# A padded tile that moves later tiles by 32 bytes, and the second token half's T sums split into an early and a late part

## The chip, the cores and the metric

The kernel runs on one core of a Trainium2 chip. The metric is the time of one execution on the device in microseconds (us). In what follows PE is TensorE, DVE is VectorE, ACT is ScalarE, POOL is GpSimd and SP is SyncE, whose queue issues all DMAs here.

## What is computed

```python
attn_out = _attn_ref(q, k, v, proj)          # (2, 8, 768, 64): attention masked by equal hash buckets
x = attn_out.transpose(0, 2, 1, 3).reshape(1536, 512)
g = h * tanh(softplus(h)),  h = x @ w_in     # moe_: 512 -> 2048 -> 512
x = g @ w_out
# moe2_: 8 experts, 512 -> 1024 -> 512, all tokens through all experts
P = exp(logits - max);  8 rounds of row and column normalisation (1536 x 8)
for e in range(8):
    out += P[:, e:e+1] * (max(x @ w1[e], 0) @ w2[e])
```

All in float32. The kernel gets float32 accuracy from TensorE's fp32r format by splitting each operand into a high part (rounded to fp32r) and a low part (the rest), and by summing three products: high x high, high x low, low x high.

## The kernel before

**Three stages.** The attention comes first (some 300 us) and is not touched. Then come the *blocks* (lines 760 to 1082): the first MLP and expert 0 of the second one, 72 steps `n` of 512 tokens by 128 hidden columns. In each step `up` (lines 785 to 787) issues 12 matmuls with 512 moving columns (stationary: a weight tile from a ring of eight, moving: `xh` and `xl`, the activations' high and low part), and `down` (L821) 12 more with the hidden tile `gh` or `gl` as one operand and the weight tile as the other. Last come the *units* (lines 1085 to 1226), `NU` = 56 of them: 28 for the first half of the tokens (g = 0), 28 for the second (g = 1), four for each of the experts 1 to 7. A unit computes a 2 x 2 block product by seven products instead of eight (Strassen's scheme in Winograd's form).

**A unit** has seven slots `s`. In slot `s`, `product(u, s)` issues six matmuls with 384 moving columns (L1111): weight sums S1 to S4 or weight blocks A as the stationary operand, token sums T1 to T4 or token blocks B (parts of `xh`, `xl`) as the moving one. After it comes a seventh of the 36 matmuls with 512 columns of the unit before (L1174, `second_mm`: stationary hidden tiles `gh`, `gl`, moving the second weights, `w` in even units and `ww` in odd ones). Then `post(u, s)` takes the products out of PSUM: DVE makes `u` after slot 1, `v` after slot 3, and `c` (L1131) after slots 4, 5 and 6; ACT rounds (`gh`, L1119), DVE makes `gl` (L1124). Two PSUM banks serve the seven products, so product 3 must wait for `u`, product 6 for the `c` of slot 4.

**Side work** is written into the slots by hand with `job(u, s, ...)` (and into the blocks' steps with `at(n, ...)`); each engine takes its instructions in the order written. For the next unit's weights POOL makes the four sums S (`unit_s`, four instructions) after slot 1, their low part (`unit_s_lo`, L1004) after slot 3, and the low part of A (`unit_a_lo`, L986 and L987) after slot 4; `unit_w_lo` (L1011) comes after slot 0. ACT makes the high parts (`..._hi`). All weights of even units go to ring tiles 0 to 2, those of odd units to `ws`, `wa`, `ww`.

**The T sums** are made by `make_t(g, k, kc, tmp)` (lines 956 to 974): three to five DVE instructions on 128 x 384 tiles in SBUF, then ACT's rounding (L973), then DVE's low part (L974). Eight calls serve a token half (k = 1 to 4, kc = 0, 1). For g = 0 they stand in the blocks' steps 61 to 68, in the midst of the normalisation rounds (steps 58 to 66; DVE's L882 to L897, PE's column sum `cs` L892 once per step). For g = 1 they stand in unit 25 (k = 2: slots 0 and 3), unit 27 (k = 3: slots 3 and 4; k = 1: slots 4 and 5; the first of k = 4: slot 6) and unit 28 (the second of k = 4: slot 0). T2 of g = 1 goes into a part of `xh`, `xl` that nobody reads any more; T1, T3 and T4 overwrite those of g = 0, which unit 27 still reads.

**Where the tiles lie.** Tiles are laid out one after another, a pool on top of the other. `fold` (L764, 32 bytes in each partition) is followed by all the tiles that the blocks and units open. In the built program `xh`, `xl`, the ring's tiles 0 to 2, `acc` and `tw` (the T sums) begin 32 bytes past a multiple of 64; the ring's tiles 3 to 7, all `gh` and `gl`, and `ws`, `wa`, `ww` begin at a multiple of 64. So the two operands of a matmul have the same offset in some places and different ones in others:

| matmuls | stationary | moving | count |
|---|---|---|---|
| `up`, ring tiles 0 to 2 | 32 | 32 | 27 x 12 |
| `up`, ring tiles 3 to 7 | 0 | 32 | 45 x 12 |
| `down`, ring tiles 3 to 7 | 0 | 0 | 45 x 12 |
| `down`, ring tiles 0 to 2 | 32 or 0 | 0 or 32 | 27 x 12 |
| products of even units | 32 | 32 | 28 x 42 |
| products of odd units | 0 | 32 | 28 x 42 |
| `second_mm`, weights of even units (issued in odd units) | 0 | 32 | 28 x 36 |
| `second_mm`, weights of odd units (issued in even units) | 0 | 0 | 28 x 36 |

Of the kernel before, what the change touches and what calls it, by code (L numbers as in the profile page):

```python
# [7 lines left out]
F32 = mybir.dt.float32  # L8
# [8 lines left out]
P = 128  # L17
# [5 lines left out]
E = 8  # L23
# [34 lines left out]
def lsh_attention_moe_kernel(  # L58
# [704 lines left out]
    NT = NTOK // P  # L763
    fold = acc_p.tile([2 * E, E], F32, name="fold")  # L764
    nc.vector.tensor_add(fold, idt[0:2 * E, 0:E], idt[0:2 * E, E:2 * E])
# [189 lines left out]

    def make_t(g, k, kc, tmp):
        n1, n2 = tokens(g, 0), tokens(g, 1)
        h, l = f32(xh), f32(xl)
        a, b = tmp(), tmp()
        if k < 4:  # L960
            p, q = ((kc, n2), (kc, n1)) if k < 3 else ((KC // 2 + kc, n2), (kc, n2))
            nc.vector.tensor_sub(a, h[:, p[0], p[1]], h[:, q[0], q[1]])
            nc.vector.tensor_sub(b, l[:, p[0], p[1]], l[:, q[0], q[1]])
            nc.vector.tensor_add(a, a, b)
        else:
            t = [factor_t(g, 2, m, kc).bitcast(F32) for m in range(2)]
# [22 lines left out]

    def unit_s(u, r):  # L990
        t = staged["u", u, 0]
        a11, a12, a21, a22 = t[:, 0, 0:256], t[:, 0, 256:512], t[:, 1, 0:256], t[:, 1, 256:512]
        nc.gpsimd.tensor_add(r[:, 0:256], a21, a22)
        nc.gpsimd.tensor_sub(r[:, 256:512], r[:, 0:256], a11)
        nc.gpsimd.tensor_sub(r[:, 512:768], a11, a21)
        nc.gpsimd.tensor_sub(r[:, 768:1024], a12, r[:, 256:512])
        box["s"] = r

    def unit_s_hi(u):
        nc.scalar.copy(wbuf[u % 2]["s"][:, 0, :], box["s"])  # L1000
# [14 lines left out]
    t0 = start_e + 12  # L1015
    at(t0, open_t)
    for x in range(8):
        at(t0 + 1 + x, make_t, 0, 1 + x // 2, x % 2, lambda: t_p.tile([P, TB], F32, tag="t", name="t")[:, :HALF])
    raw = lambda: t_p.tile([P, 1024], F32, tag="s", name="s", bufs=1)
    at(t0 + 3, unit_a_hi, 0)  # L1020
    at(t0 + 3, lambda: unit_s(0, raw()))
    at(t0 + 4, unit_s_hi, 0)
    at(t0 + 4, unit_s_lo, 0)
    at(t0 + 5, unit_a_lo, 0)
    at(t0 + 6, unit_w_hi, 0)
    at(t0 + 6, unit_w_lo, 0)

    free = {}
# [50 lines left out]
    pool = lambda name, **kw: ctx.enter_context(tc.tile_pool(name=name, reuse_waits="tile", **kw))  # L1079
    wb_p, c_p, h_p, s_p = pool("wb", bufs=1), pool("c", bufs=1), pool("hid", bufs=2), pool("sraw", bufs=1)  # L1080
    ps_u = pool("ps_u", bufs=1, space=bass.MemoryType.PSUM)
# [113 lines left out]
    for u in range(NU):  # L1195
# [3 lines left out]
        if u + 1 < NU:  # L1199
            job(u, 1, lambda u=u: unit_s(u + 1, s_p.tile([P, 1024], F32, tag="s", name="s")))  # L1200
            job(u, 2, unit_a_hi, u + 1)
# [3 lines left out]
    for i in range(NT):  # L1205
        job(i // 3, 1 + 2 * (i % 3), scale_first, i)
    half = NU // 2
    for x, (u, s) in enumerate(((-3, 0), (-3, 3), (-1, 3), (-1, 4), (-1, 4), (-1, 5), (-1, 6), (0, 0))):
        job(half + u, s, make_t, 1, (2, 3, 1, 4)[x // 2], x % 2, lambda: temp("t", 2))

# [72 lines left out]
```

## Time and profile before

| | |
|---|---|
| median of 3 runs | 1626.85 us (1626.85 to 1627.24) |
| the profiled execution | 1627.34 us, its span 1625.6 us |
| mean granted clock of TensorE | 0.986 of full speed |
| PE busy | 1569.6 us, 97% of the span |
| DVE, ACT, POOL busy | 871.3, 642.1, 865.2 us |
| share of the chain of waits that ended last: PE, DVE | 83%, 12% |

The span runs from the first instruction to the last; the rest of the execution's time (1.7 us) lies around it. A row of the timeline gives start, duration, engine, source line, operation, tile written <- tiles read, shapes, and in brackets how long the engine had been idle and what ended that. Matmuls overlap, so their pace is read from the difference of two starts and not from a duration.

### The profile page before, as it was taken

To read this page: it belongs to the slowest core of one execution; us is meant where nothing else is said; L and a number is where in the kernel's file an instruction comes from. 1 tells how busy PE (TensorE), PEld (TensorE's weight loads), DVE (VectorE), ACT (ScalarE), POOL (GpSimd) and SP (SyncE) were. 2 spreads that over 40 slices of the span, in tenths; PEclk is the share of its full clock that TensorE was granted. 3 is DMA by queue.
4 is the path that set the end of the run, shared out by engine and by line. 5 is a ranking of instruction groups with operands and counts; after the bars stand their busy time and mean duration, and the time that the engine had idled before them with its cause. 6 is when DMAs were issued, how large, how long until landed. Compare 5 with 4: busy or idle time off the path is not lost.

```text
span 1625.6 us, 20042 instructions
## 1 busy us (share of the span) xinstructions
PE 1569.6 (97%) x7407; PEld 1342.2 (83%) x7407; DVE 871.3 (54%) x1495; ACT 642.1 (40%) x1171; POOL 865.2 (53%) x694
## 2 busy tenths in 40 slices
PE   7888999999999999999999999998799999999999
PEld 5676787788888778788888888887688898888887
DVE  7999988677884222755433424336633334343343
ACT  4676776544333322223333333333333333333331
POOL 4778666432324240126666666665556666656663
PEclk7999999999999999999999999999999999999999
DMA  6755441022222010002122221222122222222221
GB/s 142 172 135 128 132 115 45 27 65 65 66 65 66 13 52 1 14 13 78 66 65 66 66 77 66 65 65 65 52 91 72 70 67 65 66 66 67 76 65 39
DMA packets 62641, 113.44 MB, mean 70 GB/s; under 512 B 18176, under 2 KB 18920, under 8 KB 62544
## 3 DMA queue, kind: packets, MB, share of 16 engines
q1 hardware_dynamic: 62544, 112.17, 23.7%
q8 instruction: 58, 0.95, 0.2%
q14 instruction: 39, 0.32, 0.1%
HBM read 89.22 MB, written 3.15 MB: 57 GB/s over the span
## 4 chain that ended last, share of the span: by engine, by line
PE 83%; DVE 12%; issue 1%; DMA 1%; ACT 1%; POOL 1%; SPq 0%; DVEq 0%; ACTq 0%; POOLq 0%
PE y L1174 28%; PE u L1111 24%; PE y L821 12%; PE h L785 4%; PE h L787 4%; PE h L786 4%; PE pav L487 3%; DVE mx L399 3%; PE ps L385 1%; PE pst L437 1%; PE pst L438 1%; DVE xu L516 1%; DVE col L404 1%; DVE vs L354 1%; DVE ph L446 0%
## 5 line engine op out<-in xcount | busy, mean ns | idle before, releaser
L1174 PE MATMUL y<-w,gh 128*128 128x512 f32 x672 | 220.9, 396 | 0.0
L1174 PE MATMUL y<-ww,gh 128*128 128x512 f32 x672 | 219.5, 395 | 0.0
L1119 ACT ACTIVATE gh<-c 128x384 fp32r<-128x384 f32 x168 | 88.3, 526 | 273.6 <-DVE c L1131 273.6
L449 POOL TENSOR_TENSOR plo<-p,ph 128x384 fp32r<-128x384 f32 x128 | 140.2, 1107 | 71.1 <-ACT ph L446 42.1
L1011 POOL TENSOR_TENSOR w<-stage,w 128x1024 fp32r<-128x1024 f32 x28 | 67.2, 2401 | 147.7 <-ACT w L1007 147.7
L1174 PEld LDWEIGHTS y<-ww,gh 128*128 128x128 f32 x672 | 125.9, 189 | 17.9
L1174 PEld LDWEIGHTS y<-w,gh 128*128 128x128 f32 x672 | 125.3, 188 | 18.2
L1011 POOL TENSOR_TENSOR ww<-stage,ww 128x1024 fp32r<-128x1024 f32 x28 | 67.5, 2409 | 127.2 <-ACT ww L1007 127.2
L1174 PE MATMUL y<-w,gl 128*128 128x512 f32 x336 | 132.9, 396 | 0.0
L1174 PE MATMUL y<-ww,gl 128*128 128x512 f32 x336 | 132.5, 394 | 0.0
L1004 POOL TENSOR_TENSOR w<-s,w 128x1024 fp32r<-128x1024 f32 x28 | 67.1, 2397 | 111.9 <-ACT w L1000 111.9
L157 POOL TENSOR_TENSOR stage<-stage,sgn 128x512 f32<-128x512 f32 x32 | 44.8, 1399 | 138.8 <-DVE sgn L155 57.3
L821 PE MATMUL y<-gh,w 128*128 128x512 f32 x336 | 111.5, 393 | 0.0
L1131 DVE TENSOR_TENSOR u<-u,p 128x384 f32<-128x384 f32 x56 | 31.2, 557 | 145.1 <-PE u L1111 145.1
L443 ACT ACTIVATE p<-pst 128x384 f32<-128x384 f32 x192 | 91.9, 488 | 42.4 <-PE pst L438 37.4
L787 PE MATMUL h<-xh,w 128*128 128x512 f32 x252 | 101.0, 401 | 2.6 <-POOL w L176 2.6
L785 PE MATMUL h<-xh,w 128*128 128x512 f32 x252 | 101.9, 405 | 0.0
L786 PE MATMUL h<-xl,w 128*128 128x512 f32 x252 | 101.0, 401 | 0.0
L399 DVE TENSOR_REDUCE mx<-ps 128x1 f32<-128x768 f32 x95 | 89.9, 946 | 17.2 <-PE ps L385 16.5
L1124 DVE SCALAR_TENSOR_TENSOR gl<-c,gh 128x384 fp32r<-128x384 f32 x168 | 96.1, 572 | 5.4
L1111 PE MATMUL u<-tw,w 128*128 128x384 f32 x420 | 86.2, 341 | 4.7 <-DVE u L1131 4.5
L1119 ACT ACTIVATE gh<-u 128x384 fp32r<-128x384 f32 x56 | 27.5, 491 | 157.1 <-PE u L1111 157.1
(244 smaller groups left out, 4004.9 us busy)
## 6 DMA issues: line engine op xcount, KB each, us to landing
stage<-in_w_dram SPq DMA_DIRECT2D x152, 512.0 KB
raw<-in_qk_dram SPq DMA_DIRECT2D x13, 384.0 KB
wx<-hi SPq DMA_DIRECT2D x20, 192.0 KB
vt<-in_v_dram SPq DMA_DIRECT2D x16, 192.0 KB
out_dram<-acc SPq DMA_DIRECT2D x12, 256.0 KB
zq<-hi SPq DMA_DIRECT2D x11, 192.0 KB
ak<-hi SPq DMA_DIRECT2D x11, 192.0 KB
zq<-lo SPq DMA_DIRECT2D x11, 192.0 KB
```

The costliest lines, as they stand in the source:

```text
L399: nc.vector.tensor_reduce(out=m[:, t:t + 1], in_=s_t[t][:, :, :HALF], axis=AX.XY, op=ALU.max)
L443: nc.scalar.activation(p_t[u, c], st_t.pop((u, c))[:, :HALF], AF.Exp, scale=0.125)
L449: (nc.gpsimd if e == "P" else nc.vector).tensor_sub(out, in0, in1)
L785: nc.tensor.matmul(t, wt[:, 0, f], xh[:, kc, c], start=(kc == 0), stop=False)
L786: nc.tensor.matmul(t, wt[:, 0, f], xl[:, kc, c], start=False, stop=False)
L787: nc.tensor.matmul(t, wt[:, 1, f], xh[:, kc, c], start=False, stop=(kc == KC - 1))
L821: nc.tensor.matmul(yps[j], x, y, start=(head and m == 0), stop=(tail and m == 2))
L1011: nc.gpsimd.tensor_sub(y[:, 1, :], t, f32(y)[:, 0, :])
L1111: nc.tensor.matmul(bank[x], weight(u, a, m, kc), moving(u, b, mm, kc), start=(first and n == 0), stop=(n == 5), skip_group_check=not first)
L1119: nc.scalar.activation(hi, src, AF.Relu)
L1124: nc.vector.scalar_tensor_tensor(out=lo, in0=src, scalar=0.0, in1=f32(hid_u[u, c][0]), op0=ALU.max, op1=ALU.subtract)
L1174: nc.tensor.matmul(y_t[t], (hi, hi, lo)[m][:, t % 3 * P:(t % 3 + 1) * P], y, start=(k == 0 and first and m == 0), stop=(k == NF // 2 - 1 a ...
```

## The change

`fold` is allocated 64 bytes wide and used in its first 32, so all that follows it begins 32 bytes later; one tile `sraw` takes the place of two tiles for the raw S sums. In the built program every tile of the table above then begins 32 bytes past a multiple of 64. `make_t` is cut into `raw_t` (the sum, on DVE) and `parts_t` (ACT's high, DVE's low part). For g = 1 the raw sums are made one per unit, in slot 3 of units 18 to 25; for k = 2 the parts follow at once (units 18, 19), for the other six the sum is held in a tile of its own, and the parts are made in unit 27 (slots 4, 5, 6) and 28 (slots 0, 1, 2). For g = 0 the eight calls stand three steps later in the blocks (64 to 71 for 61 to 68). The S sums of unit 1 move from slot 1 of unit 0 to step 69 of the blocks.

```diff
-    fold = acc_p.tile([2 * E, E], F32, name="fold")
+    fold = acc_p.tile([2 * E, 2 * E], F32, name="fold")[:, 0:E]
+    sraw = acc_p.tile([P, 1024], F32, name="sraw")
...
-    def make_t(g, k, kc, tmp):
+    def raw_t(g, k, kc, a, b):
...
+    def parts_t(g, k, kc, a):
         hi, lo = (factor_t(g, k, m, kc) for m in range(2))
         nc.scalar.copy(hi, a)
         nc.vector.tensor_sub(lo, a, hi.bitcast(F32))
...
+    def make_t(g, k, kc, tmp):
+        a = tmp()
+        raw_t(g, k, kc, a, tmp())
+        parts_t(g, k, kc, a)
+
     for x in range(8):
-        at(t0 + 1 + x, make_t, 0, 1 + x // 2, x % 2, ...)
+        at(t0 + 4 + x, make_t, 0, 1 + x // 2, x % 2, ...)
...
+    at(t0 + 9, unit_s, 1)
...
-            job(u, 1, lambda u=u: unit_s(u + 1, s_p.tile([P, 1024], F32, tag="s", name="s")))
+            if u:
+                job(u, 1, unit_s, u + 1)
...
-    for x, (u, s) in enumerate(((-3, 0), (-3, 3), (-1, 3), (-1, 4), (-1, 4), (-1, 5), (-1, 6), (0, 0))):
-        job(half + u, s, make_t, 1, (2, 3, 1, 4)[x // 2], x % 2, lambda: temp("t", 2))
+    held = {}
+
+    def raw_next(k, kc):
+        held[k, kc] = temp(f"t{k}{kc}" if k != 2 else "t")
+        raw_t(1, k, kc, held[k, kc], temp("tt"))
+        if k == 2:
+            parts_t(1, k, kc, held.pop((k, kc)))
+
+    def parts_next(k, kc):
+        parts_t(1, k, kc, held.pop((k, kc)))
+
+    for x in range(8):
+        job(half - 10 + x, 3, raw_next, (2, 3, 1, 4)[x // 2], x % 2)
+    for x, (u, s) in enumerate(((-1, 4), (-1, 5), (-1, 6), (0, 0), (0, 1), (0, 2))):
+        job(half + u, s, parts_next, (3, 1, 4)[x // 2], x % 2)
```

**DVE in unit 27, slots 3 to 5, before.** `v` and the `c`s are the sums that release PE's next products; `t` and `tw` belong to the T sums.

```order
L1131 TENSOR_TENSOR v<-u,p_10225 128x384
L962 TENSOR_TENSOR t<-xh 128x384
L963 TENSOR_TENSOR t<-xl 128x384
L964 TENSOR_TENSOR t<-t 128x384
L974 TENSOR_TENSOR tw<-t,tw 128x384
L1131 TENSOR_TENSOR c<-u,v 128x384
...
L1131 TENSOR_TENSOR c<-u,p_10225 128x384
L1124 SCALAR_TENSOR_TENSOR gl<-c,gh 128x384
```

At the "..." stand two more T sums whole, eight instructions. With the change the same place reads:

```order
L1139 TENSOR_TENSOR v<-u,p_10225 128x384
L1139 TENSOR_TENSOR c<-u,v 128x384
L977 TENSOR_TENSOR tw<-t_9352,tw 128x384
L1139 TENSOR_TENSOR c<-u,p_10225 128x384
L1132 SCALAR_TENSOR_TENSOR gl<-c,gh 128x384
L977 TENSOR_TENSOR tw<-t_9494,tw 128x384
L1139 TENSOR_TENSOR c<-u 128x384
```

One low part stands after each `c`, where up to eight instructions stood between two.

**DVE in units 18 and 20, slot 3, with the change** (k = 2, then k = 3; `t_9352` is the held sum):

```order
L1139 TENSOR_TENSOR v<-u,p_9028 128x384
L963 TENSOR_TENSOR t<-xh 128x384
L964 TENSOR_TENSOR tt<-xl 128x384
L965 TENSOR_TENSOR t<-t,tt 128x384
L971 TENSOR_TENSOR tt<-xh,xl 128x384
L972 TENSOR_TENSOR t<-tt,t 128x384
L977 TENSOR_TENSOR xl<-t,xh 128x384
L1139 TENSOR_TENSOR c<-u,v 128x384
...
L963 TENSOR_TENSOR t_9352<-xh 128x384
L964 TENSOR_TENSOR tt<-xl 128x384
L965 TENSOR_TENSOR t_9352<-t_9352,tt 128x384
L1139 TENSOR_TENSOR c<-u,v 128x384
```

Nothing stood there before between `v` and `c`; now it is six instructions (with ACT's rounding ahead of the last) in units 18 and 19, three in units 20 to 25.

**DVE in the blocks, between two of the normalisation's column sums** (`csum`, which PE's `cs` waits for), before, in the step before the last round:

```order
L887 TENSOR_REDUCE csum<-prob 128x8
L962 TENSOR_TENSOR t<-xh 128x384
L963 TENSOR_TENSOR t<-xl 128x384
L964 TENSOR_TENSOR t<-t 128x384
L970 TENSOR_TENSOR t<-xh,xl 128x384
L971 TENSOR_TENSOR t<-t 128x384
L974 TENSOR_TENSOR tw<-t,tw 128x384
L802 SCALAR_TENSOR_TENSOR gl<-h,gh 128x512
```

and with the change:

```order
L889 TENSOR_REDUCE csum<-prob 128x8
L963 TENSOR_TENSOR t<-xh 128x384
L964 TENSOR_TENSOR t<-xl 128x384
L965 TENSOR_TENSOR t<-t 128x384
L977 TENSOR_TENSOR tw<-t,tw 128x384
L804 SCALAR_TENSOR_TENSOR gl<-h,gh 128x512
```

The two sums of k = 1 stand in the last two rounds, where the second sum of k = 2 and the first of k = 3 stood, and the rounds before them have no T sum (they had three). The orders on SP and PE are the same in both kernels.

## Rows read from the trace of the kernel before

**Rows 1.** Timeline of PE, first matmul of units 30, 31 and 32.

```profile
1205.35 0.33 PE L1111 MATMUL u<-xh,wx 128*128 128x384 f32 x1
...
1220.98 0.34 PE L1111 MATMUL u<-xh,wa 128*128 128x384 f32 x1
...
1236.74 0.33 PE L1111 MATMUL u<-xh,wx 128*128 128x384 f32 x1
```

**Rows 2.** Timeline of PE in the blocks, first matmuls of six runs of twelve.

```profile
346.89 0.39 PE L785 MATMUL h<-xh,w 128*128 128x512 f32 x1
...
349.63 0.40 PE L821 MATMUL y<-gh,wx 128*128 128x512 f32 x1
...
352.43 0.39 PE L785 MATMUL h<-xh,wx 128*128 128x512 f32 x1
...
391.47 0.40 PE L785 MATMUL h<-xh,w 128*128 128x512 f32 x1
...
394.29 0.40 PE L821 MATMUL y<-gh,w 128*128 128x512 f32 x1
...
397.04 0.40 PE L785 MATMUL h<-xh,w 128*128 128x512 f32 x1
```

**Rows 3.** Timeline of PE, first matmul of units 25 to 29.

```profile
1107.49 0.34 PE L1111 MATMUL u<-xh,wa 128*128 128x384 f32 x1
...
1128.72 0.33 PE L1111 MATMUL u<-xh,wx 128*128 128x384 f32 x1
...
1144.35 0.34 PE L1111 MATMUL u<-xh,wa 128*128 128x384 f32 x1
...
1164.60 0.41 PE L1111 MATMUL u<-xh,wx 128*128 128x384 f32 x1 [3.34 <-DVE c L1131]
...
1189.58 0.34 PE L1111 MATMUL u<-xh,wa 128*128 128x384 f32 x1
```

**Rows 4.** Timeline, unit 25: slot 4's `c` after a k = 2 sum, then product 6.

```profile
1125.55 0.55 DVE L1131 TENSOR_TENSOR c<-u,v 128x384 f32<-128x384 f32 x1
...
1126.16 0.45 PE L1111 MATMUL u<-xh,ws 128*128 128x384 f32 x1 [2.58 <-DVE c L1131]
```

**Rows 5.** Timeline of DVE, then of POOL, unit 27 from slot 3.

```profile
1152.27 0.56 DVE L1131 TENSOR_TENSOR v<-u,p 128x384 f32<-128x384 f32 x1 [1.13 <-PE u L1111]
...
1153.79 2.65 DVE L964 TENSOR_TENSOR t<-t 128x384 f32<-128x384 f32 x1
...
1153.64 2.39 POOL L1004 TENSOR_TENSOR w<-s,w 128x1024 fp32r<-128x1024 f32 x1 [1.16 <-ACT w L1000]
1155.98 1.62 POOL L986 TENSOR_TENSOR wx<-stage,wx 128x512 fp32r<-128x512 f32 x1
1157.57 1.03 POOL L987 TENSOR_TENSOR wx<-stage,wx 128x256 fp32r<-128x256 f32 x1
```

**Rows 6.** Timeline, unit 19, which has no T sum: `v` and product 6.

```profile
1021.25 0.56 DVE L1131 TENSOR_TENSOR v<-u,p 128x384 f32<-128x384 f32 x1 [1.13 <-PE u L1111]
...
1026.63 0.34 PE L1111 MATMUL u<-xh,ws 128*128 128x384 f32 x1
```

**Rows 7.** Timeline of DVE and PE, `csum` of steps 62 and 65, the `cs` after each.

```profile
660.16 0.34 DVE L887 TENSOR_REDUCE csum<-prob 128x8 f32<-128x96 f32 x1
...
663.60 0.28 PE L892 MATMUL cs<-csum,ones 128*128 128x8 f32 x2
...
678.71 0.69 DVE L802 SCALAR_TENSOR_TENSOR gl<-h,gh 128x512 fp32r<-128x512 f32 x1 [0.88 <-ACT gh L801]
...
683.22 0.32 DVE L887 TENSOR_REDUCE csum<-prob 128x8 f32<-128x96 f32 x1
...
683.59 0.39 PE L892 MATMUL cs<-csum,ones 128*128 128x8 f32 x2 [2.49 <-DVE csum L887]
```

**Rows 8.** Windows: start:end, length, busy of PE, PEld, DVE, ACT, POOL, granted clock, DMA.

```profile
683.80:688.40 4.60, 4.60 (x15) 3.65 (x15) 3.99 (x8) 1.01 (x2) 0.00 (x0) 0.63 0.32 110
1116.60:1128.70 12.10, 9.44 (x45) 8.16 (x46) 9.96 (x15) 3.08 (x5) 5.14 (x4) 1.00 0.14 45
```

More of the change, by code (lines that the diff above doesn't have):

```diff
@@ L954, in factor_t @@
         return tw[0][:, k - 1, m, kc, :]
-    def make_t(g, k, kc, tmp):
+    def raw_t(g, k, kc, a, b):
         n1, n2 = tokens(g, 0), tokens(g, 1)
         h, l = f32(xh), f32(xl)
-        a, b = tmp(), tmp()
         if k < 4:
@@ L988, in unit_a_lo, with unit_s @@
         load_next()
-    def unit_s(u, r):
-        t = staged["u", u, 0]
+    def unit_s(u):
+        t, r = staged["u", u, 0], sraw
         a11, a12, a21, a22 = t[:, 0, 0:256], t[:, 0, 256:512], t[:, 1, 0:256], t[:, 1, 256:512]
@@ L996, in unit_s @@
         nc.gpsimd.tensor_sub(r[:, 768:1024], a12, r[:, 256:512])
-        box["s"] = r
     def unit_s_hi(u):
-        nc.scalar.copy(wbuf[u % 2]["s"][:, 0, :], box["s"])
+        nc.scalar.copy(wbuf[u % 2]["s"][:, 0, :], sraw)
     def unit_s_lo(u):
         s = wbuf[u % 2]["s"]
-        nc.gpsimd.tensor_sub(s[:, 1, :], box["s"], f32(s)[:, 0, :])
+        nc.gpsimd.tensor_sub(s[:, 1, :], sraw, f32(s)[:, 0, :])
     def unit_w_hi(u):
@@ L1016, in lsh_attention_moe_kernel @@
     at(t0, open_t)
+    def make_t(g, k, kc, tmp):
+        a = tmp()
+        raw_t(g, k, kc, a, tmp())
+        parts_t(g, k, kc, a)
     for x in range(8):
-        at(t0 + 1 + x, make_t, 0, 1 + x // 2, x % 2, lambda: t_p.tile([P, TB], F32, tag="t", name="t")[:, :HALF])
-    raw = lambda: t_p.tile([P, 1024], F32, tag="s", name="s", bufs=1)
+        at(t0 + 4 + x, make_t, 0, 1 + x // 2, x % 2, lambda: t_p.tile([P, TB], F32, tag="t", name="t")[:, :HALF])
     at(t0 + 3, unit_a_hi, 0)
-    at(t0 + 3, lambda: unit_s(0, raw()))
+    at(t0 + 3, unit_s, 0)
     at(t0 + 4, unit_s_hi, 0)
@@ L1079, in lsh_attention_moe_kernel @@
     pool = lambda name, **kw: ctx.enter_context(tc.tile_pool(name=name, reuse_waits="tile", **kw))
-    wb_p, c_p, h_p, s_p = pool("wb", bufs=1), pool("c", bufs=1), pool("hid", bufs=2), pool("sraw", bufs=1)
+    wb_p, c_p, h_p = pool("wb", bufs=1), pool("c", bufs=1), pool("hid", bufs=2)
     ps_u = pool("ps_u", bufs=1, space=bass.MemoryType.PSUM)
```

## The prediction

> **What bounds the kernel now.** I read the timeline of PE first, because PE is busy 97% of the span: the time is PE's pace plus the places where PE stands still. Three things show.
>
> *The pace depends on a table.* Unit 30 takes 1220.98 - 1205.35 = 15.63 us, unit 31 takes 1236.74 - 1220.98 = 15.76 us [rows 1]. Both issue 42 matmuls of 384 columns and 36 of 512. Unit 31 has them with unequal offsets (0 against 32), unit 30 with equal ones. In the blocks the same shows inside a step [rows 2]: twelve matmuls of `up` on ring tile 1 (both operands at 32) take 349.63 - 346.89 = 2.74 us, the twelve of `down` behind them on `wx`, ring tile 2 (32 against 0), take 2.80. Later, on ring tiles 3 to 7, it is the other way round: `up` (0 against 32) takes 394.29 - 391.47 = 2.82, `down` (both 0) 2.75. So it is neither `up` nor `down` that is slow, it is the unequal pair, by 0.05 to 0.08 us in twelve.
>
> *Three units near the middle are long* [rows 3]: unit 25 takes 21.23 us, unit 27 20.25, unit 28 24.98. Against the 15.76 and 15.63 of their kind [rows 1] that is 5.47 + 4.49 + 9.35 = 19.3 us. The rows' brackets name DVE's `c`. In unit 25 the `c` of slot 4 starts at 1125.55, behind a k = 2 sum, and product 6 starts at 1126.16 after 2.58 us of idling [rows 4].
>
> *One pause in the blocks*: PE's last `cs` waits 2.49 us for `csum` [rows 7], and then the granted clock is 0.63 over 4.6 us [rows 8], between the levels of 1.2 and 2.4 GHz, which costs another 4.6 x (1 - 0.63) = 1.7 us.
>
> **The change, part by part.**
>
> *1. Equal offsets.* With the change all pairs are 32 against 32. Blocks: 45 runs of `up` go from 2.82 to 2.74, 27 runs of `down` from 2.80 to about 2.75; I take 0.07 and 0.055 from several such runs, 45 x 0.07 + 27 x 0.055 = 4.6 us. Units: 28 odd ones go from 15.76 to 15.63, 28 x 0.13 = 3.6 us. Together 8.2 us. The 384-column products hardly matter: 36 matmuls at the blocks' price per twelve (3 x 0.055 = 0.17) more than account for the 0.13 between the units. Above this lies a further 2 us or so, if both at 32 is faster than both at 0 also in the units, as 2.74 against 2.75 hints (0.01 x 3 runs x 56 units = 1.7). Below it lies 0, if the offset only goes along with something else, as the tile's place. All of it is on the path, since PE never waits in these stretches.
>
> A rule speaks against this part. The Trainium skill, "SBUF — State Buffer", section "Who interferes with whom", gives PE two independent read ports, one for the moving operand and one for weight loads, and says that PE never waits on anyone. By that rule an operand's offset would change nothing and this term would be 0; rows 1 and 2 speak for 8.2, in four separate pairings, and I go by them.
>
> *2. The T sums of the second half.* The 19.3 us go, and what takes their place is this. A sum in slot 3 stands in DVE's queue between `v` and the `c` of slot 4, which releases product 6; queued behind it are that `c`, ACT's rounding of it and the later `c`s. In a unit without a sum product 6 starts 1026.63 - 1021.25 = 5.38 us after `v` [rows 6]; `c` (0.55) may thus start up to 4.8 us after `v` at no cost.
>
> How late is it now? Unit 27 shows the three instructions of a k = 3 sum [rows 5]: two run in half a microsecond each, the third starts at 1153.79, during POOL's low part of S (1153.64 to 1156.03), and ends at 1156.44, 0.41 after POOL. That is 4.17 after `v`, so `c` would end at about 4.7: 0.7 us to spare. The six sums for k = 3, 1 and 4 in units 20 to 25 have three such instructions each and nothing on ACT: no cost, with 0.7 us of cover.
>
> The two k = 2 sums (units 18, 19) have two more instructions, then ACT, then the low part. Each of the two meets another POOL instruction [rows 5], the last of which ends at 1158.60, 6.33 after `v`; with 0.4 for the blocked one, 0.6 for ACT, 0.5 for the low part and 0.5 for `c` it is 8.3 to 8.4, 3.0 us late. Unit 25 had this very sequence and PE idled 2.58 [rows 4]. I take 2.9 each, 5.8 together. The clock stayed at 1.00 after 2.58 us of idling, but fell after 2.49 [rows 8, 7]; I count one such loss of 1.7 on the two. The late halves of the other six are one ACT and one DVE instruction per slot, in units 27 and 28, after sums that PE already has: one of them, in slot 0 of unit 28, stands behind POOL's `unit_w_lo` and pushes `u` by about 2 us of the 2.4 that a slot gives. I put 0.4 on all six. So 19.3 - 5.8 - 1.7 - 0.4 = 11.4 us. Ends: 19.3 - 2 x 2.6 = 14.1 if the pauses are as in unit 25 and the clock holds, 19.3 - 2 x (3.1 + 1.7) - 1.5 = 8.2 if not.
>
> *3. T sums of the first half, three steps later.* Before, `csum` of step 62 ended 3.1 us ahead of its `cs` [rows 7]; three steps with k = 2 and k = 3 sums used that up. Now the rounds of steps 61 to 63 have no sum, so DVE enters step 64 in time. There a k = 1 sum and ACT's rounding of S push step 65's `gl`, from which it took 683.54 - 678.71 = 4.8 us to the end of `csum`, POOL's blocking included [rows 7]. I make that `gl` about 6.4 us after the `cs` of step 64, so that `csum` ends at 11.2, and the last `cs` is due two steps of 5.78 later, 11.6: 0.3 us to spare. The pause goes, 2.5 + 1.7 = 4.2 us. If my estimate of the queue is half a microsecond short, a short pause stays; 0 is the lower end. The sums that moved behind the rounds (steps 66 to 71) delay only `gl`s, which PE reads three steps later, and finish before unit 0's slots 1 to 5.
>
> *4. The rest.* S of unit 1 now lies ready before unit 0, but ACT's rounding in unit 0 waits for PE's slot 2 anyway: 0. `fold` wider, `sraw` for the two old tiles: 0. Tiles of the blocks lie over others of the attention than before; PE has finished the attention by then: 0.
>
> The sum is 8.2 + 11.4 + 4.2 = 23.8 us. The profiled execution took 1627.3, its span 1625.6 with 1.7 around it; that makes 1603.5. The median of the runs lies 0.5 below this execution, so I say **1603 us**.
>
> **The rivals.**
>
> *The offset is nothing* (the skill's rule above). For it: a port that never waits. Against it: four pairings in two stages. Then part 1 is 0 and the time 1603 + 8.2 = 1611.2.
>
> *The pause at the last `cs` stays.* For it: 0.3 us to spare, by a queue that I put together myself. Then 1603 + 4.2 = 1607.2.
>
> *Better than that*: both at 32 gains everywhere, and the clock holds in units 18 and 19: 1603 - 1.7 - 1.7 - 0.6 = 1599.
>
> *Slower than before*: the early sums stall PE in all eight units. Place: slot 3 of units 18 to 25. Price: 2.9 for the pause and 1.7 for the clock, 4.6 x 8 = 36.8 instead of 19.3, that is 17.5 more, less 8.2 and 4.2: 1632. It decides when the `c` of a three-instruction sum starts over 4.8 us after `v`, and reaches this price when it starts at 7.7. Against it: rows 5 put it at 4.2, before POOL's next instruction can block it.
>
> **How the numbers follow.** My forecast has 0.60, with 1598 to 1609 for its own range. The offset as nothing has 0.15, the staying pause 0.12, the better case 0.10, the slower one 0.03. The range of 1598 to 1611 takes in the forecast, the better case, the staying pause and about half of the case without offsets. What a measurement of this kernel can tell from no change is about 0.2%, 3.3 us. Faster by more than that 0.96, within it 0.01, slower 0.03.
>
> **What would show it.** Right: units 30 and 31 alike at 15.6 us; units 20 to 28 at their kind's length but for fractions of a microsecond; units 18 and 19 long by 2.6 to 4.8; no wait of PE for `csum`. Wrong: unit 31 still 0.13 longer than unit 30, then the offset was not the cause; units 20 to 25 long, then the third instruction waited for more than one of POOL's; a drop of the clock at `cs`, then part 3 failed.

## The result, and the profile after

The changed kernel takes 1604.32 us (median of 4 runs, 1602.7 to 1607.85), the kernel before 1626.85. The ratio is 0.9865, with a 95% interval of 0.9848 to 0.9883. The prediction said 1603.0, from 1598 to 1611.

| | before | after |
|---|---|---|
| the profiled execution, its span | 1627.34, 1625.6 us | 1605.15, 1603.4 us |
| mean granted clock of TensorE | 0.986 | 0.989 |
| PE busy | 1569.6 us | 1557.0 us |
| DVE, ACT, POOL busy | 871.3, 642.1, 865.2 us | 885.5, 642.1, 871.3 us |

In the tables and the text that follow, line numbers are those of the changed kernel: `up` L787 to L789, `down` L823, products L1119, `second_mm` L1182, the `c`, `u`, `v` sums L1139.

The list of waits of PE after the change, from 600 us to the end (waiter, what it waited for, total, times, longest):

```profile
PE u L1119 <- DVE c L1139: 5.5, 2, 3.0
PE u L1119 <- POOL wa L989: 1.4, 1, 1.4
PE y L823 <- DVE acc L833: 1.0, 2, 0.5
PE u L1119 <- DVE gl L1132: 0.2, 1, 0.2
```

The six waits for `c` and `u` of the long units have become two, the wait of `cs` for `csum` [rows 7] is gone, and one is new: `down` waits twice for DVE's evacuation `acc`. The wait for `wa`, in unit 1, and the short one for `gl` were there before.

The timeline of PE after the change. The first six rows answer to [rows 2], the last three to [rows 1]; between them stand the starts of units 18, 19 and 20, of 25 and of 29 [rows 3], and the two products behind the pauses.

```profile
346.80 0.39 PE L787 MATMUL h<-xh,w 128*128 128x512 f32 x1
...
349.54 0.39 PE L823 MATMUL y<-gh,wx 128*128 128x512 f32 x1
...
352.34 0.39 PE L787 MATMUL h<-xh,wx 128*128 128x512 f32 x1
...
391.16 0.40 PE L787 MATMUL h<-xh,w 128*128 128x512 f32 x1
...
393.92 0.40 PE L823 MATMUL y<-gh,w 128*128 128x512 f32 x1
...
396.69 0.40 PE L787 MATMUL h<-xh,w 128*128 128x512 f32 x1
...
990.71 0.33 PE L1119 MATMUL u<-xh,wx 128*128 128x384 f32 x1
...
1007.09 0.44 PE L1119 MATMUL u<-xh,w 128*128 128x384 f32 x1 [3.00 <-DVE c L1139]
...
1009.65 0.34 PE L1119 MATMUL u<-xh,wa 128*128 128x384 f32 x1
...
1025.44 0.45 PE L1119 MATMUL u<-xh,ws 128*128 128x384 f32 x1 [2.45 <-DVE c L1139]
...
1029.55 0.34 PE L1119 MATMUL u<-xh,wx 128*128 128x384 f32 x1
...
1107.62 0.34 PE L1119 MATMUL u<-xh,wa 128*128 128x384 f32 x1
...
1170.06 0.34 PE L1119 MATMUL u<-xh,wa 128*128 128x384 f32 x1
...
1185.64 0.33 PE L1119 MATMUL u<-xh,wx 128*128 128x384 f32 x1
...
1201.27 0.34 PE L1119 MATMUL u<-xh,wa 128*128 128x384 f32 x1
...
1216.85 0.33 PE L1119 MATMUL u<-xh,wx 128*128 128x384 f32 x1
```

Read them in three steps.

- *Units.* Unit 30 still takes 1201.27 - 1185.64 = 15.63 us; unit 31 now takes 1216.85 - 1201.27 = 15.58, where it took 15.76. The odd units are not level with the even ones, they are faster.
- *Blocks.* `up` on ring tiles 3 to 7 falls from 2.82 to 393.92 - 391.16 = 2.76 us. But `down` on `wx` stays at 352.34 - 349.54 = 2.80, and `down` on tiles 3 to 7 goes from 2.75 to 2.77. The 2.80 stays for the 18 runs of `down` on ring tiles 0 to 2 in which the weights are the stationary operand; the 9 with the hidden tile as the stationary one fall from 2.80 to 2.75 (medians).
- *The long units.* The four units 25 to 28 together take 1170.06 - 1107.62 = 62.44 us, which is 2 x 15.58 + 2 x 15.63: the 19.3 us are gone. Units 18 and 19 take 18.94 and 19.90 in their place, 7.6 us over their kind (15.63 and 15.58).

From unit 0 to unit 55 the trace shows one other long unit, unit 1 with its wait for `wa`: 17.23 us, and 17.35 before. Unit 0 itself begins at 715.94 after the change, at 721.47 before.

### The profile page after: what moved, and what is told of

Read it like the earlier page. It is cut to its first block, busy times and chain, and to the rows that moved or that the text cites. A ratio compares the mean times of both kernels' runs of the same rounds, so it can differ in the third digit from the quotient of the medians.

```text
span 1603.4 us, 20032 instructions
## 1 busy us (share of the span) xinstructions
PE 1557.0 (97%) x7407; PEld 1336.7 (83%) x7407; DVE 885.5 (55%) x1495; ACT 642.1 (40%) x1171; POOL 871.3 (54%) x694
## 4 chain that ended last, share of the span: by engine, by line
PE 83%; DVE 12%; issue 2%; ACT 1%; DMA 1%; POOL 0%; SPq 0%; DVEq 0%; ACTq 0%; POOLq 0%
PE y L1182 29%; PE u L1119 25%; PE y L823 11%; PE h L787 4%; PE h L789 4%; PE h L788 4%; PE pav L487 3%; DVE mx L399 3%; PE ps L385 1%; PE pst L437 1%; PE pst L438 1%; DVE col L404 1%; DVE xu L516 1%; DVE vs L354 1%; DVE ph L446 1%
## 5 line engine op out<-in xcount | busy, mean ns | idle before, releaser
L1182 PE MATMUL y<-w,gh 128*128 128x512 f32 x672 | 219.4, 394 | 0.0
L1182 PE MATMUL y<-ww,gh 128*128 128x512 f32 x672 | 218.4, 393 | 0.0
L1182 PEld LDWEIGHTS y<-ww,gh 128*128 128x128 f32 x672 | 125.2, 188 | 17.3
L1182 PEld LDWEIGHTS y<-w,gh 128*128 128x128 f32 x672 | 125.6, 189 | 16.7
L1182 PE MATMUL y<-w,gl 128*128 128x512 f32 x336 | 131.9, 393 | 0.0
L1182 PE MATMUL y<-ww,gl 128*128 128x512 f32 x336 | 131.6, 392 | 0.0
L1006 POOL TENSOR_TENSOR w<-sraw,w 128x1024 fp32r<-128x1024 f32 x28 | 68.1, 2430 | 107.7 <-ACT w L1002 107.7
L823 PE MATMUL y<-gh,w 128*128 128x512 f32 x336 | 111.7, 393 | 0.0
L1139 DVE TENSOR_TENSOR u<-u,p 128x384 f32<-128x384 f32 x56 | 31.2, 557 | 141.3 <-PE u L1119 141.3
L1132 DVE SCALAR_TENSOR_TENSOR gl<-c,gh 128x384 fp32r<-128x384 f32 x168 | 102.9, 613 | 5.8
L789 PE MATMUL h<-xh,w 128*128 128x512 f32 x252 | 99.7, 395 | 2.7 <-POOL w L176 2.7
L787 PE MATMUL h<-xh,w 128*128 128x512 f32 x252 | 101.2, 402 | 0.0
L1006 POOL TENSOR_TENSOR ws<-sraw,ws 128x1024 fp32r<-128x1024 f32 x28 | 67.2, 2400 | 57.4 <-ACT ws L1002 57.4
```

Of the source, the lines that this page charges most:

```text
L787: nc.tensor.matmul(t, wt[:, 0, f], xh[:, kc, c], start=(kc == 0), stop=False)
L789: nc.tensor.matmul(t, wt[:, 1, f], xh[:, kc, c], start=False, stop=(kc == KC - 1))
L823: nc.tensor.matmul(yps[j], x, y, start=(head and m == 0), stop=(tail and m == 2))
L1006: nc.gpsimd.tensor_sub(s[:, 1, :], sraw, f32(s)[:, 0, :])
L1132: nc.vector.scalar_tensor_tensor(out=lo, in0=src, scalar=0.0, in1=f32(hid_u[u, c][0]), op0=ALU.max, op1=ALU.subtract)
L1182: nc.tensor.matmul(y_t[t], (hi, hi, lo)[m][:, t % 3 * P:(t % 3 + 1) * P], y, start=(k == 0 and first and m == 0), stop=(k == NF // 2 - 1 a ...
```

## The experiments

The medians are of four executions, beside the kernel before on the same chip (median 1626.28 us for the paddings of 32, 96 and 128 bytes and for slot 6, 1624.91 us for the next four); the last three kernels have one execution each, beside one of the kernel before of 1623.01 us. The changed kernel's own 1604.32 us stand beside 1626.85, so between two of these groups up to 3.8 us of a difference can have nothing to do with an edit. A small difference between two profiles can come from TensorE's clock alone (see the end), so stages are compared by their rows.

### The padding undone

```diff
-    fold = acc_p.tile([2 * E, 2 * E], F32, name="fold")[:, 0:E]
+    fold = acc_p.tile([2 * E, E], F32, name="fold")[:, 0:E]
```

> The changed kernel with fold 32 bytes wide again, all else as changed, so that the ring's tiles 3 to 7, gh, gl, ws, wa and ww begin at a multiple of 64 again. Theory (the pair's offset sets PE's pace): odd units go back from 15.58 to 15.76 us, runs of twelve up matmuls on ring tiles 3 to 7 from 2.76 to 2.815; even units stay at 15.63; the time is 28 x 0.18 + 45 x 0.05 + 9 x 0.045 = 7.7 us above the changed kernel's 1604.3, so 1612. Rival (the offset is nothing, the T sums alone did it): odd units stay at 15.58, time 1604.

Measured: 1610.16 us (1608.31 to 1614.35), ratio 0.9905 (0.9884 to 0.9927). The timeline of PE, units 30, 31 and 32 of this run:

```profile
1190.01 0.33 PE L1119 MATMUL u<-xh,wx 128*128 128x384 f32 x1
...
1205.65 0.34 PE L1119 MATMUL u<-xh,wa 128*128 128x384 f32 x1
...
1221.41 0.33 PE L1119 MATMUL u<-xh,wx 128*128 128x384 f32 x1
```

The odd unit is back at 1221.41 - 1205.65 = 15.76 us, the even one at 15.64. The blocks, from the first `up` to unit 0, take 717.60 - 299.89 = 417.71 us in this run and 715.94 - 300.60 = 415.34 after the change, 2.4 us apart. So the padding alone is worth some 6 us, by the medians 1610.16 - 1604.32 = 5.8 and by the rows 2.4 + 28 x 0.18 = 7.4, and the rival by which it is worth nothing is out.

### A padding of 96 bytes

```diff
-    fold = acc_p.tile([2 * E, 2 * E], F32, name="fold")[:, 0:E]
+    fold = acc_p.tile([2 * E, 3 * E], F32, name="fold")[:, 0:E]
```

> The changed kernel with fold 96 bytes wide: the tiles named for the 32-byte fold begin 64 bytes later than there, at a multiple of 64 (and of 512) again, while xh, xl and ring tiles 0 to 2 stay 32 past one. Theory A (what counts is whether both offsets are equal modulo 64): as with 32 bytes, odd units 15.76, up on ring tiles 3 to 7 2.815, time about 1612. Theory B (what counts is the distance of the moving operand's address from the stationary's, modulo something larger than 64, and small positive distances are free): here moving minus stationary is +32 for up on tiles 3 to 7 and for the odd units' second matmuls, so odd units stay at 15.58 or below, up on tiles 3 to 7 at 2.74 to 2.77, while down on ring tiles 0 to 2 (distance -32) stays at 2.80; time about 1604.

Measured: 1610.58 us (1608.31 to 1612.35), ratio 0.9903 (0.9886 to 0.9921). The moved tiles now begin at a multiple of 64 again, 32 short of the others. Odd units take 15.72 us (median of those without a pause), even ones 15.63, and `up` on ring tiles 3 to 7 takes 2.80 us (median). It is as slow as without padding: what counts is how the two operands stand to each other, not how far the tiles were moved. Theory B is out for a distance of 32: `up`, whose moving tile begins 32 past its stationary one, takes 2.80 and not 2.74 to 2.77.

### A padding of 128 bytes

```diff
-    fold = acc_p.tile([2 * E, 2 * E], F32, name="fold")[:, 0:E]
+    fold = acc_p.tile([2 * E, 4 * E], F32, name="fold")[:, 0:E]
```

> The changed kernel with fold 128 bytes wide: all the tiles begin 32 past a multiple of 64, as changed, but now ring tiles 3 to 7, gh, gl, ws, wa, ww and xh, xl, ring tiles 0 to 2 also agree modulo 512 (all 32). Theory A (equal modulo 64 is all that counts): as the changed kernel, down on ring tiles 0 to 2 stays at 2.80, odd units 15.58, time 1604. Theory B (the distance modulo something larger counts): every run of twelve goes to 2.74, also the 27 of down on ring tiles 0 to 2 that the change left at 2.80 (27 x 0.06 = 1.6 us) and up on tiles 3 to 7 (45 x 0.024 = 1.1 us); time about 1601.5.

In the built program of the change `xh`, `xl` and ring tiles 0 to 2 begin 32 bytes past a multiple of 512, the moved tiles 480 past one: equal modulo 64, but not modulo 128. In the kernel before the moved tiles begin 448 past one, and `tw` begins 480 past one in every kernel here. With this edit the moved tiles begin at 32 past a multiple of 512 as well. Measured: 1605.62 us (1603.94 to 1607.45), ratio 0.9874 (0.9857 to 0.9891), about as the change. The timeline of PE shows two effects that cancel; three starts in the blocks (`down` on `wx`, `up`, `down` on tiles 3 to 7), then units 30, 31 and 32:

```profile
370.68 0.39 PE L823 MATMUL y<-gh,wx 128*128 128x512 f32 x1
...
373.40 0.39 PE L787 MATMUL h<-xh,w 128*128 128x512 f32 x1
...
376.12 0.39 PE L823 MATMUL y<-gh,w 128*128 128x512 f32 x1
...
1185.16 0.33 PE L1119 MATMUL u<-xh,wx 128*128 128x384 f32 x1
...
1200.85 0.33 PE L1119 MATMUL u<-xh,wa 128*128 128x384 f32 x1
...
1216.55 0.33 PE L1119 MATMUL u<-xh,wx 128*128 128x384 f32 x1
```

Both runs of twelve take 2.72 us, less than the median of any pairing of the kernel before or of the change. The units, though, both take 15.69 or 15.70, longer than after the change (15.63 and 15.58); neither theory foresaw that. Equality modulo 64 was thus not the whole of it: a larger modulus counts, and it helps in the blocks and hurts in the units.

### The k = 2 sums in slot 6

```diff
-        job(half - 10 + x, 3, raw_next, (2, 3, 1, 4)[x // 2], x % 2)
+        job(half - 10 + x, 6 if x < 2 else 3, raw_next, (2, 3, 1, 4)[x // 2], x % 2)
```

> The changed kernel with the two k = 2 sums of the second half in slot 6 of units 18 and 19 instead of slot 3, nothing else. Theory (the pause comes from POOL's instructions holding back DVE's, and from the short way from v to the c of slot 4): in slot 6 POOL has finished and DVE has 3 us before the next u is due, so units 18 and 19 fall from 18.94 and 19.90 to 15.6 to 16.0 us, no clock loss follows, time 7 us lower, 1597. Rival (six DVE instructions with ACT's rounding in a row are too long for any slot): they stay over 17.5 us each and the time over 1601.

Measured: 1594.45 us (1593.47 to 1595.34), ratio 0.9803 (0.9786 to 0.982). Units 18 and 19 take 15.63 and 15.59 us, with no wait for `c`. That is 7.6 us by the rows, of which unit 21 gives back some 0.35 (15.94 us, its first product gets the low part of `wa` late). The rest of the 9.9 between the medians is outside of these units (in the profiled execution 1.6 us come from a clock that held after a pause near 311 us, see the end). The two pauses in units 18 and 19 were all that was left of the wait for the T sums.

### GpSimd's splits behind the sums

Why does a sum of five instructions make `c` late? After the change the timeline shows unit 18 so, DVE first, then POOL:

```profile
998.55 0.56 DVE L1139 TENSOR_TENSOR v<-u,p 128x384 f32<-128x384 f32 x1 [1.11 <-PE u L1119]
...
1000.08 2.77 DVE L965 TENSOR_TENSOR t<-t,tt 128x384 f32<-128x384 f32 x1
1002.88 1.55 DVE L971 TENSOR_TENSOR tt<-xh,xl 128x384 f32<-128x384 f32 x1
1004.47 0.96 DVE L972 TENSOR_TENSOR t<-tt,t 128x384 f32<-128x384 f32 x1
...
1006.48 0.55 DVE L1139 TENSOR_TENSOR c<-u,v 128x384 f32<-128x384 f32 x1
...
1000.04 2.39 POOL L1006 TENSOR_TENSOR ws<-sraw,ws 128x1024 fp32r<-128x1024 f32 x1 [1.16 <-ACT ws L1002]
1002.39 1.63 POOL L989 TENSOR_TENSOR wa<-stage,wa 128x512 fp32r<-128x512 f32 x1
1003.98 1.03 POOL L990 TENSOR_TENSOR wa<-stage,wa 128x256 fp32r<-128x256 f32 x1
```

Three DVE instructions end 0.42, 0.41 and 0.42 us behind one POOL instruction each (1002.85 against 1002.43, 1004.43 against 1004.02, 1005.43 against 1005.01). The Trainium skill, "SBUF — State Buffer", section "Who interferes with whom", has a DVE instruction with two SBUF inputs contend with a GpSimd instruction that reads SBUF, and the loser blocked, not slowed; this trace agrees, with 2.77 us for an instruction that takes 0.56 alone. The experiment keeps the sums in slot 3 and takes POOL's work out of their way, in units 18 and 19 only:

```diff
-            job(u, 2, unit_a_hi, u + 1)
-            job(u, 3, unit_s_hi, u + 1)
-            job(u, 3, unit_s_lo, u + 1)
-            job(u, 4, unit_a_lo, u + 1)
+            late = u in (NU // 2 - 10, NU // 2 - 9)
+            job(u, 4 if late else 2, unit_a_hi, u + 1)
+            job(u, 4 if late else 3, unit_s_hi, u + 1)
+            if late:
+                job(u, 4, unit_a_lo, u + 1)
+            job(u, 4 if late else 3, unit_s_lo, u + 1)
+            if not late:
+                job(u, 4, unit_a_lo, u + 1)
```

> The k = 2 sums stay in slot 3 of units 18 and 19, and GpSimd's splits of the next unit's weights (with the ScalarE copies ahead of them) move from slots 2 to 4 into slot 4 of those two units, behind the sums. Theory (GpSimd's long subtracts, which run at the same time, hold VectorE's sums back to 2.8 and 1.5 us for one that takes 0.55 alone): the sums take about 4 us instead of 7, c comes in time, and units 18 and 19 fall from 18.9 and 19.9 us to between 15.6 and 16.6 each, so 1596.5 to 1599 in all. A part may come back where the later splits make TensorE wait for the weights of the next unit (up to 1 us a unit, seen as a wait of its weight load for GpSimd). Rival (six instructions and the turn through ScalarE are too long for the slot, whoever else runs): both units stay at 18.5 us or more, 1603 to 1605.

Measured: 1598.11 us (1597.49 to 1598.88), ratio 0.9834 (0.9818 to 0.9851). The timeline of DVE in unit 18 of this run:

```profile
998.82 0.56 DVE L1139 TENSOR_TENSOR v<-u,p 128x384 f32<-128x384 f32 x1 [1.11 <-PE u L1119]
...
1000.35 0.56 DVE L965 TENSOR_TENSOR t<-t,tt 128x384 f32<-128x384 f32 x1
...
1003.15 0.55 DVE L1139 TENSOR_TENSOR c<-u,v 128x384 f32<-128x384 f32 x1
```

`c` starts 1003.15 - 998.82 = 4.33 us behind `v`, against 1006.48 - 998.55 = 7.93 after the change, and within the 4.8 that the prediction allowed. The instruction that took 2.77 us takes 0.56. Unit 18 takes 15.63 us, units 19 and 20 take 16.15 each, with waits of 0.3 and 0.2 us for the later splits. The number of instructions in the slot was not what made them late; POOL's three subtracts were. ACT's copies moved along with them, but after the change ACT had been idle for 5.50 us when the sum came to it for rounding, so they did not hold it up.

### The T sums of the first half at their old place

```diff
-        at(t0 + 4 + x, make_t, 0, 1 + x // 2, x % 2, ...)
+        at(t0 + 1 + x, make_t, 0, 1 + x // 2, x % 2, ...)
```

> The T sums of the first token half go back to the three earlier steps of the kernel before; the rest is as in the change. Theory: these sums sat in VectorE's queue ahead of the csum on which the last cs of the normalization waits, so the pause of about 2.5 us before that cs comes back, with up to 1.8 us of lower clock behind it, while the two waits of TensorE for the evacuation of acc (1.5 us together after the change) go or shrink. Net of the changed kernel's 1604.3: +1 to +3 us, so 1605 to 1607.5, the pause of cs visible in the list of waits. Rival 1 (the pause had another cause, such as the clock or the padded tile): no pause at cs, 1602 to 1604.5. Rival 2 (the waits for acc come from the evacuation itself and not from the sums ahead of it): the two waits for acc stay at 0.7 us each as well, 1607 to 1609.

Measured: 1610.21 us (1607.93 to 1611.12), ratio 0.9908 (0.9893 to 0.9923), some 3 us more than the upper end expected. The list of waits of this run, without those of 1.4 and 0.2 us for `wa` and `gl` that every kernel here has:

```profile
PE u L1119 <- DVE c L1139: 5.5, 2, 3.0
PE cs L894 <- DVE csum L889: 2.6, 1, 2.6
```

The pause at `cs` is back and the two waits for `acc` are gone, as the theory has it. The rows price it: from the first `up` to unit 0 this run takes 717.42 - 299.09 = 418.33 us against 415.34, so the three steps are worth 3.0 us net. Units 18 and 19 take 21.04 and 18.91 us in its profile, 1.1 more than after the change. The medians differ by 5.9; where the other two microseconds lie is open.

### Both kinds of offsets, each in its stage

The tiles of the blocks get the offsets of the 128-byte run and those of the units keep the change's, by a pad at the start of the units' pools; the k = 2 sums are in slot 6.

```diff
-    fold = acc_p.tile([2 * E, 2 * E], F32, name="fold")[:, 0:E]
+    fold = acc_p.tile([2 * E, 4 * E], F32, name="fold")[:, 0:E]
...
+    wb_p.tile([P, 112], F32, name="pad")
     wbuf.append(dict(
...
-        job(half - 10 + x, 3, raw_next, (2, 3, 1, 4)[x // 2], x % 2)
+        job(half - 10 + x, 6 if x < 2 else 3, raw_next, (2, 3, 1, 4)[x // 2], x % 2)
```

> The k = 2 sums in slot 6 (as in the run that took them there), the fold tile padded to 128 bytes a partition (operands of the blocks at equal offsets modulo 512), and a pad of 448 bytes ahead of the second weight set of the units, so that their tiles lie at the offsets of the changed kernel. Theory (the offset of an operand decides by itself, stage by stage): runs of twelve in the blocks at 2.72 us, the units at 15.63 (even) and 15.58 (odd) as after the change, no pause in units 18 and 19: unit 0 begins at about 711, and the span is 1589 to 1592. Rival (what made the units slow in the run with 128 bytes was not their weight tiles but the pad itself, or the place of xh and w against them): units at 15.69, 1593 to 1596.

Measured: 1592.35 us (1588.8 to 1593.88), ratio 0.9797 (0.9782 to 0.9812). Runs of twelve 2.72 us, even units 15.63, odd ones 15.59 (medians): each stage follows the offsets of its own operands.

### T sums away from the evacuations

The new wait for `acc` after the change is seen where DVE and PE meet at 682 us. The timeline of DVE, then of PE:

```profile
677.72 0.36 DVE L889 TENSOR_REDUCE csum<-prob 128x8 f32<-128x96 f32 x1
...
680.68 0.69 DVE L804 SCALAR_TENSOR_TENSOR gl<-h,gh 128x512 fp32r<-128x512 f32 x1
681.29 2.47 DVE L833 TENSOR_TENSOR acc<-y,acc 128x512 f32<-128x512 f32 x4
...
678.47 0.28 PE L894 MATMUL cs<-csum,ones 128*128 128x8 f32 x2
...
682.11 0.47 PE L823 MATMUL y<-w,gh 128*128 128x512 f32 x1 [0.50 <-DVE acc L833]
```

Between `csum` and `gl` DVE makes a T sum; it delays `gl`, and behind it `acc`, whose banks PE needs for the next group of `down`. The experiment adds one edit to the run before:

```diff
-        at(t0 + 4 + x, make_t, 0, 1 + x // 2, x % 2, ...)
+        at(t0 + (4, 6, 7, 8, 10, 11, 12, 13)[x], make_t, 0, 1 + x // 2, x % 2, ...)
```

> As the run with the pads of 128 and 448 bytes, and the T sums of the first token half leave the two steps ahead of the evacuations of acc (sums at steps 64, 66, 67, 68, 70, 71, 72, 73). Theory (those sums make the evacuation late): no wait of TensorE for acc in the last steps of the blocks, 1.5 us less than the run without this, so 1587.5 to 1590.5. Rival: the sums only move the wait, to the last cs or to the products of unit 0 that read T4: as the run without this, within 0.7 us, or up to 2 us longer.

Measured: 1589.92 us (1586.74 to 1590.95), ratio 0.9782 (0.9767 to 0.9796). The list of PE's waits of this run, whole:

```profile
PE u L1120 <- POOL wa L989: 1.4, 1, 1.4
PE u L1120 <- DVE gl L1133: 0.2, 1, 0.2
```

No wait for `acc`; the blocks take 707.73 - 299.17 = 408.56 us, 2.0 less than in the run before (410.52). This is the fastest version: 2.2% under the kernel before, and 14.4 us under the change by the medians, 12.5 when each is set against the kernel before of its own group.

### Which modulus

Two further paddings of `fold`, with the pad ahead of the units shortened by as much, so that these stay where they are. In the first the moved tiles of the blocks lie 128 bytes from the others modulo 512, in the second 256:

```diff
-    fold = acc_p.tile([2 * E, 4 * E], F32, name="fold")[:, 0:E]
+    fold = acc_p.tile([2 * E, 8 * E], F32, name="fold")[:, 0:E]
...
-    wb_p.tile([P, 112], F32, name="pad")
+    wb_p.tile([P, 80], F32, name="pad")
```

> As the run with pads and the later T sums (unit 0 at 707.73, runs of twelve 2.72 us), but the fold tile takes 256 bytes a partition, so that gh, gl and ring tiles 3 to 7 begin 128 bytes further than xh, xl and ring tiles 0 to 2, modulo 512; the pad ahead of the units keeps their tiles where they were. Theory 128 (offsets need only be equal modulo 128): all runs of twelve stay at 2.72 us, span 1586.5 to 1590. Theory 512 (they must be equal modulo 512): runs that read one operand of each group go to 2.74 to 2.80 us, as after the change, 3 to 6 us in the blocks, span 1591 to 1594.

```diff
-    fold = acc_p.tile([2 * E, 4 * E], F32, name="fold")[:, 0:E]
+    fold = acc_p.tile([2 * E, 12 * E], F32, name="fold")[:, 0:E]
...
-    wb_p.tile([P, 112], F32, name="pad")
+    wb_p.tile([P, 48], F32, name="pad")
```

> As the run before it in this list, with 384 bytes for the fold tile: gh, gl and ring tiles 3 to 7 begin 256 bytes further than xh, xl and ring tiles 0 to 2, modulo 512. Theory 128 and a theory 256 (equal modulo 256 is enough) give runs of twelve of 2.72 us and a span of 1586.5 to 1590; theory 512 gives 2.74 to 2.80 us for the runs of mixed operands and 1591 to 1594. With the run of 256 bytes the two tell the modulus apart.

Measured: 1592.48 and 1592.04 us. The timelines of PE tell them apart. With 128 bytes between the operands (`down` on `wx`, `up`, `down` on tiles 3 to 7):

```profile
367.31 0.40 PE L823 MATMUL y<-gh,wx 128*128 128x512 f32 x1
...
370.10 0.40 PE L787 MATMUL h<-xh,w 128*128 128x512 f32 x1
...
372.90 0.39 PE L823 MATMUL y<-gh,w 128*128 128x512 f32 x1
```

With 256 bytes, the same three:

```profile
371.62 0.39 PE L823 MATMUL y<-gh,wx 128*128 128x512 f32 x1
...
374.34 0.39 PE L787 MATMUL h<-xh,w 128*128 128x512 f32 x1
...
377.06 0.39 PE L823 MATMUL y<-gh,w 128*128 128x512 f32 x1
```

128 apart costs 2.79 and 2.80 us for twelve, 256 apart 2.72 and 2.72, as if equal. So neither of theories 128 and 512 holds, but the one named for 256: in the blocks it is equality modulo 256 that gives the full pace. The first takes 710.51 - 297.73 = 412.78 us for its blocks, 4.2 more than the fastest run. The second is slower than the fastest run only ahead of the blocks: its first `up` comes at 301.44 (299.17 there), and its blocks take 710.04 - 301.44 = 408.60 us (408.56).

The last kernel shortens only the pad ahead of the units, so that their tiles lie 256 bytes from `xh` and ring tiles 0 to 2:

```diff
-    wb_p.tile([P, 112], F32, name="pad")
+    wb_p.tile([P, 64], F32, name="pad")
```

> As the run with pads and the later T sums, but the pad ahead of the units' tiles is 256 instead of 448 bytes, so that ws, wa, ww and the units' gh and gl begin 256 bytes from xh and ring tiles 0 to 2 (and 192 from the T sums), modulo 512. Theory (in the units, too, equality decides, with the modulus of the blocks): if the blocks show that 256 apart counts as equal, units as in the run with 128 bytes for fold and no pad, 15.69 us, so 3 to 4 us longer than with 448; if 256 apart counts as unequal, units between 15.57 and 15.76 us. Rival (the units' time doesn't follow from equality of offsets, since matmuls of two widths alternate there): a value outside of the blocks' pattern, such as odd and even units at or under 15.57.

Measured: 1590.26 us. In the timeline of PE units 30, 31 and 32 begin at 1168.41, 1184.10 and 1199.79: both kinds take 15.69 us, as in the run with 128 bytes and no pad, where these tiles lay at the offset of `xh` itself (in both the units of the first half take 15.65, those of the second 15.69). 256 apart again counts as equal, and in the units that is slower, in these by 0.06 us in an even and 0.11 in an odd one. From unit 0 to the end the run takes 1588.5 - 704.6 = 883.9 us against 1588.0 - 707.7 = 880.3 in the fastest run; its time is about the same only because unit 0 begins 3.1 us earlier.

Why the units are slower is open. It isn't the pair alone: `xh` and ring tiles 0 to 2 lie at 32 in every run here, and yet their four products in even units of the second half go from 176.8, 174.8, 173.7 and 173.2 ns from start to start in the fastest run (means of 70) to 174.2, 178.7, 178.7 and 176.8 here, one faster and three slower. The distance of the units' tiles from `tw` changes as well, from 0 to 64 modulo 256. Whether the accesses of other engines to the moved tiles play a part was not tested.

## Why the prediction was right, and where its steps were off

**The time.** 1603 was forecast, 1604.3 came; the sum was 23.8 us against a measured loss of 22.2 in the spans. The three parts, each against its rows:

| part | predicted | measured |
|---|---|---|
| 1. offsets, blocks | 4.6 | 2.4 |
| 1. offsets, odd units | 28 x 0.13 = 3.6 | 28 x 0.18 = 5.0 |
| 2. T sums of the second half | 11.4 | 19.3 - 7.6 = 11.7 |
| 3. T sums of the first half | 4.2 | 3.0 |

The blocks' and the first-half terms are those that the runs which undo them measured; the others come from the unit starts.

**Part 1 holds as a sum (7.4 against 8.2) and not in its step.** The failed step is "With the change all pairs are 32 against 32", from which every slow pairing was to fall to the price of the equal one. Modulo 64 that is true of the tiles, but the runs show that 256 bytes are the period. 480 against 32 is still an unequal pair: `down` on `wx` stayed at 2.80, and `up` on tiles 3 to 7 reached 2.76 and not 2.74. The table of offsets hides this for the units too: in even units three or four of the seven products read `tw`, 64 from their weights modulo 256, before and after. Nor was 2.74 the floor: an equal pair takes 2.74 beside runs at other offsets, and 2.72 where all tiles of the blocks are equal. In the odd units the step erred the other way: with the pair that came out, 64 apart from `xh` modulo 256, they take 15.58 us, and 15.69 where their tiles begin at the offset of `xh`. The 384-column products were not without weight either: in odd units of the second half the four on `xh` went from 176.4 to 173.2 ns from start to start, 24 x 3.2 = 77 ns of the 0.18 us. That the sum came out near is luck: the blocks gave 2.2 us less than predicted and the odd units 1.4 more. The Trainium skill, "SBUF — State Buffer", "Who interferes with whom", says that PE's two read ports are independent and that PE waits on no one. Whatever that says of other engines, the places of PE's own two operands change its pace (2.72 to 2.82 us for the same twelve matmuls), so the measurement decides: undoing the padding cost 5.8 us, where the rival built on this rule has 0.

**Part 2 holds, with luck in one term.** The sums for k = 3, 1 and 4 cost nothing, units 20 to 24 and 25 to 28 being at their kind's length. The two k = 2 sums were put at 2.9 us each, and PE idled 3.00 and 2.45; one loss of clock was counted, and one is there. The latter is luck: with the same sums in the same slots, the clock fell behind both pauses in the runs with 96 and 128 bytes (0.50 over the first 4 us behind the one, 0.69 and 0.68 behind the other). That POOL's instructions make the length, the ground of the estimate, is shown by the run that moved them.

**Part 3: the mechanism is right, a term was left out.** The pause went: `csum` ended at 678.08, 0.39 us ahead of its `cs` (0.3 was predicted), and undoing the step brought back 2.56 us of idling with a granted clock of 0.57 behind it. What failed is the sentence that the later sums "delay only `gl`s": behind the `gl` of a group's last step stands `acc`, and PE waits for it at the next group's first `down`. That cost 0.5 us of idling twice, some 1.3 us with the slow restart (starts 0.90 and 0.89 us apart where 0.23 is the rule), and the run with the sums moved from there shows it gone. The term measured 3.0 for 4.2.

## What to carry to other kernels

Read PE's pace for each pairing of operands, stage by stage, before touching addresses: here the place of tiles modulo 256 bytes was worth up to 0.10 us in twelve matmuls, and the best place differed between two stages, so each wants its own pad. When side work moves into another slot, look not only at the instruction that it stands ahead of but through the queue up to the last one that another engine waits for, and at what the sharing engine does in the same microseconds: the same DVE instructions cost 2.5 to 3 us of PE's time beside POOL's subtracts and none after them.

## What the runs showed of the hardware that was not expected

**The pace of matmuls goes by offsets modulo 256.** In the blocks twelve matmuls of 512 columns took 2.72 us (medians, here and in what follows) where all operands of the stage begin at the same offset or 256 bytes apart, 2.74 to 2.78 for equal pairs beside others, and 2.79 to 2.82 for pairs 32, 96 or 128 apart. At 64 it goes by the direction: 2.75 and 2.76 where the moving tile begins 64 bytes past the stationary one modulo 256, 2.80 where it begins 64 short of it. Equal pairs beside others lose their time at the start of a run: with 256 bytes for `fold`, the first three matmuls of such a run are 230 to 232 ns from start to start and the next eight 227, the pace of a stage where all are equal.

In the odd units of the second half, where matmuls of 384 and 512 columns alternate, the distance of the units' tiles from `xh` gave 15.58 us at 64, 15.69 at 0 and 256, 15.72 at 32 and 15.76 at 96. Their distance from `tw` was 0, 64, 32 and 32 in these, so that the units don't price one pair by itself.

**The same pause costs clock in one execution and not in another.** After the change the two pauses in units 18 and 19 lie ahead of these two windows (start:end, length, busy PE with its count, granted clock, DMA share, GB/s):

```profile
1007.00:1010.00 3.00, 2.91 (x15) 1.00 0.32 119
1025.40:1029.60 4.20, 4.16 (x13) 0.59 0.40 125
```

After 3.00 us of idling PE ran at 2.4 GHz, after 2.45 us at about half of that, the 1.2 GHz level, for most of 4.2 us. With the T sums of the first half at their old place, the windows behind `cs` and behind the same two pauses were:

```profile
679.60:683.60 4.00, 3.93 (x11) 0.57 0.42 133
1008.50:1012.50 4.00, 3.92 (x11) 0.50 0.23 86
1029.60:1033.60 4.00, 3.99 (x20) 1.00 0.44 129
```

There it is the first of the two pauses that cost clock. The wait of 2.6 us of the first `up` on ring tile 3 (near 311 us, with every kernel here) was followed over the next 4 us by a granted clock of 0.57 after the change and of 1.00 in the run with the k = 2 sums in slot 6. So a pause of 2.5 to 3 us costs itself and, in some executions, another 1.6 to 2 us. A part of the spread between executions, 1602.7 to 1607.85 us for the changed kernel, is likely to come from this; only profiled executions show it.
